# Attention and feed-forward on one core: weighted sums next to the scores, feed-forward work behind them, batches begun a third of a group later, no dummies in batch 0

## Chip, cores, metric

One core of a Trainium2 chip. The metric is device time in microseconds (us); each kernel was run several times and medians are quoted with their ranges. A profile shows one execution, and its span is some 1.8 us shorter than the time of the same run.

## The reference

```python
# q, k, v: (8, 12, 448, 64); batch 8, 12 heads, 448 positions, 64 per head
scores = scale * q @ k^T
m = max(scores);  e = exp(scores - m)
attn = e / (sum(e) + exp(-m) + 1e-9)
x = (attn @ v), heads side by side            # (3584, 768)
h = maximum(maximum(x @ w1, x @ w2), x @ w3)  # three up projections
out = h @ w_out                               # (3584, 768), float32
```

## The kernel before

A *group* is four heads of one batch, so a batch has three groups and there are 24. A group's scores come in seven units, visited in three *visits* of 2, 2 and 3 units. In the first two visits of group i the weighted sums (`av`, e times v) of group i-1 are done too. ScalarE (ACT) takes the exponentials, VectorE (DVE) divides (`xn`) and a DMA transposes the result (`xT`). The feed-forward of a batch is cut into pieces (six matmuls each, or twelve narrower ones); `fill` emits pieces between the attention work, so that TensorE (PE) has work while exponentials run. Batch 0 has nothing to fill with at first: its queries are split into an "E" part (with dummy matmuls) and an "O" part (filled with feed-forward of the E rows).

PSUM, where PE writes, is two pools: three large tiles of two banks for scores and weighted sums, two small ones of one bank for feed-forward pieces:

```python
ps_s = tile_pool(name="ps_s", bufs=3, space=PSUM)   # tiles [128, 2, 512] fp32
ps_b = tile_pool(name="ps_b", bufs=2, space=PSUM)   # tiles [128, 512] fp32
```

The main loop:

```python
for i in range(3, NI):
    ...  # DMA transposes of q, k for group i+2, loads
    if i >= 7 and i % 3 == 1:
        add_batch(i // 3 - 1)              # next batch's pieces, at visit 0
    ...
    for vi, units in enumerate(visits):
        ...
        scores(i, (i + 1) % NEB, units)
        if vi < 2:
            av_tail(i - 1, pj, vi, ws)
        if vi == 0:
            per = share()
        fill(per / 6)
        if vi < 2:
            av_main(i - 1, pj, vi, ws)
        if vi == 1:
            ...
                x_transpose_dma(i - 1)     # xn -> xT, issued from the SP queue
        ...
        fill(per / 6)
        if vi == 2 and i + 1 < PE_QK:
            transpose_pe(i + 1, 0, nc.vector)
            transpose_pe(i + 1, 1, nc.vector)
    if i + 2 < NI and i + 2 >= PE_QK:
        shift_q(i + 2, nc.gpsimd)          # waits for the DMA transpose of q
    prep_v(i, nc.vector if i < PE_QK else nc.gpsimd)   # v for group i's weighted sums
```

The softmax here doesn't subtract the row's maximum and nothing guards it: scores larger than these inputs give would overflow.

## Time and profile before

| | before |
|---|---|
| median of the first three runs | 364.44 us (363.95 to 368.81) |
| span of the profiled run | 360.7 us |
| PE busy | 336.8 us |
| first 448-column scores (group 3) | 46.73 us |
| first matmul of batch 1's feed-forward | 90.54 us |

In the profile page the span is cut into 40 slices (9.0 us each); a digit is the busy share in tenths, PEclk the clock granted to PE. Two rows of the kernel before:

```profile
PE   8899978886999979999799999999999999999994
PEclk9999999999999999999899999999999999999998
```

Apart from the last slice, the lowest PE digits lie in the first ten slices; later single digits 7 stand at borders of batches, and the one 8 in the clock row before the end follows such a border. The chain that ended last, of the same page, by line:

```profile
PE p_i L389 46%; PE op_ps L412 11%; PE avp L319 10%; PE stp L262 9%; DMA xT<-xn 6%; PE avp L302 2%; DMA QT<-ld_q 2%; DMA ld_v<-in_v_dram 2%; ACT e L282 1%; PE trT L170 1%; DVE QT L191 1%; DVE xn L335 1%; DVE KT L189 1%; POOL QT L207 1%; PE warm L155 1%
```

Most is PE's own work (p_i: up projections, op_ps: output projection, avp: weighted sums, stp: scores). What is not is foremost the DMA transpose xT<-xn with 6%. GpSimd's (POOL's) timeline of the kernel before (start us, us, instruction, count, idle before it and what ended it) shows the order behind the 2.6 us wait on vt:

```profile
86.43 2.34 POOL L207 COPY QT<-QT 64x384 f16<-64x384 f16 x4 [8.14 <-DMA QT<-ld_q]
88.83 0.82 POOL L345 COPY vx<-ld_v 128x768 f16<-128x768 f16 x1
89.60 0.29 POOL L347 COPY vt<-ld_v 64x128 f16<-64x128 f16 x1
```

`prep_v` (L345, L347) stands behind `shift_q` (L207), which waited 8.14 us for a DMA that PE did not yet need.

### The profile page before, as it was taken

What the parts mean: (1) busy time and instruction counts of PE and PEld (TensorE: products, weight loads), DVE (VectorE), ACT (ScalarE), POOL (GpSimd) and SP (SyncE); (2) the same over time, 40 slices, a digit from 0 to 9 for tenths busy, and PEclk for the clock granted to TensorE, in tenths of its full rate; (3) what the DMA queues carried; (4) which work ended last, traced back from release to release, by engine and by line L of the source; (5) the groups of instructions that cost most, each with busy time, mean ns of one, the idle gap of its engine ahead of it and who ended that gap; (6) DMA issues with size and microseconds to landing.
All of it is one profiled execution on the core that took longest, in us unless ns stands there. A gap on an engine that the chain in (4) does not pass through costs nothing.

```text
span 360.7 us, 9768 instructions
## 1 busy us (share of the span) xinstructions
PE 336.8 (93%) x4168; PEld 199.3 (55%) x4168; DVE 190.9 (53%) x423; ACT 147.2 (41%) x174; POOL 136.7 (38%) x241
## 2 busy tenths in 40 slices
PE   8899978886999979999799999999999999999994
PEld 3557757753555645555455645555555655565552
DVE  2665556653554636554355545555554655565553
ACT  3672355556245244455243443545445255400000
POOL 8733433153805806273246334636192600000000
PEclk9999999999999999999899999999999999999998
DMA  7999997979999995999986997999999251115006
GB/s 107 198 208 206 206 200 75 125 123 236 135 117 102 168 222 99 115 136 115 204 110 89 143 170 184 131 102 155 199 147 116 69 148 29 32 31 131 2 8 167
DMA packets 89499, 47.42 MB, mean 131 GB/s; under 512 B 58224, under 2 KB 85872, under 8 KB 89456
## 3 DMA queue, kind: packets, MB, share of 16 engines
q0 software_dynamic: 29392, 22.03, 47.4%
q1 hardware_dynamic: 60064, 24.78, 39.6%
q8 instruction: 32, 0.52, 0.7%
q14 instruction: 11, 0.09, 0.1%
HBM read 44.04 MB, written 11.01 MB: 153 GB/s over the span
## 4 chain that ended last, share of the span: by engine, by line
PE 80%; DMA 10%; DVE 4%; POOL 2%; ACT 1%; issue 1%; ACTq 0%; POOLq 0%; DVEq 0%
PE p_i L389 46%; PE op_ps L412 11%; PE avp L319 10%; PE stp L262 9%; DMA xT<-xn 6%; PE avp L302 2%; DMA QT<-ld_q 2%; DMA ld_v<-in_v_dram 2%; ACT e L282 1%; PE trT L170 1%; DVE QT L191 1%; DVE xn L335 1%; DVE KT L189 1%; POOL QT L207 1%; PE warm L155 1%
## 5 line engine op out<-in xcount | busy, mean ns | idle before, releaser
L282 ACT ACTIVATE e<-stp 128x896 f16<-128x896 f32 (+4 forms) x171 | 144.8, 903 | 162.5 <-PE stp L262 162.4
L389 PE MATMUL p_i<-xT,w 128*128 128x448 f16 (+2 forms) x972 | 179.7, 333 | 5.8 <-DMA xT<-xn 5.3
L389 PEld LDWEIGHTS <-w 128*128 128x128 f16 x972 | 87.8, 98 | 71.5 <-issue 13.0
L400 DVE TENSOR_TENSOR hT<-hT,p_i 128x448 f16<-128x448 f16 (+2 forms) x96 | 59.6, 621 | 65.5 <-PE p_i L389 65.5
L207 POOL COPY QT<-QT 64x384 f16<-64x384 f16 (+1 forms) x72 | 39.9, 555 | 125.7 <-DMA QT<-ld_q 120.0
L412 PE MATMUL op_ps<-w,hT 128*128 128x384 f16 x336 | 58.8, 326 | 0.0
L262 PE MATMUL stp<-QT,KT 64*64 64x448 f16 (+2 forms) x756 | 49.1, 339 | 4.4 <-DVE QT L191 2.6
L398 DVE CAST hT<-p_i 128x448 f16<-128x448 f32 (+2 forms) x48 | 30.0, 625 | 40.3 <-PE p_i L389 40.3
L419 DVE TENSOR_SCALAR o_sb<-op_ps 128x384 f32<-128x384 f32 x56 | 31.1, 556 | 29.6 <-PE op_ps L412 29.6
L319 PEld LDWEIGHTS <-e 128*128 128x128 f16 x1152 | 42.3, 98 | 6.8 <-issue 0.2
L319 PE MATMUL avp<-vx,e 128*128 128x65 f16 x1152 | 45.4, 194 | 0.0
L412 PEld LDWEIGHTS <-hT 128*128 128x128 f16 x336 | 31.0, 98 | 21.8 <-issue 2.2
L335 DVE TENSOR_TENSOR xn<-avp,rb 128x512 f16<-128x512 f32 (+1 forms) x54 | 34.1, 632 | 1.9
L262 PEld LDWEIGHTS <-KT 64*64 64x64 f16 x756 | 15.1, 105 | 33.1 <-issue 23.9
L302 PEld LDWEIGHTS <-e 64*64 64x64 f16 x768 | 14.9, 107 | 14.5 <-issue 4.7
L302 PE MATMUL avp<-vt,e 64*64 64x65 f16 x768 | 16.3, 193 | 5.7 <-POOL vt L347 2.6
L103 POOL DMA_DIRECT2D ld_k<-in_k_dram x25 | 17.8, 713 | 4.8 <-DMA w<-in_moe_w_out_dram 1.5
L103 POOL DMA_DIRECT2D ld_q<-in_q_dram x24 | 17.8, 742 | 3.9 <-DMA w<-in_moe_w_dram 1.2
L329 DVE TENSOR_SCALAR rb<-avp 128x8 f32<-128x8 f32 (+1 forms) x54 | 8.9, 164 | 15.0 <-PE avp L319 11.0
L116 POOL DMA_DIRECT2D ld_v<-in_v_dram x24 | 15.2, 634 | 3.4 <-DMA w<-in_moe_w_out_dram 1.6
L113 POOL DMA_DIRECT2D ld_v<-in_v_dram x24 | 15.1, 631 | 2.3 <-DVE xT L368 1.5
L345 POOL COPY vx<-ld_v 128x768 f16<-128x768 f16 x18 | 14.8, 822 | 1.7 <-POOL vt L348 0.7
(32 smaller groups left out, 90.5 us busy)
## 6 DMA issues: line engine op xcount, KB each, us to landing
out_dram<-o_sb SPq DMA_DIRECT2D x56, 192.0 KB, 3.2
ld_v<-in_v_dram POOLq DMA_DIRECT2D x48, 128.0 KB, 5.0
ld_q<-in_q_dram POOLq DMA_DIRECT2D x24, 224.0 KB, 8.0
ld_k<-in_k_dram POOLq DMA_DIRECT2D x23, 224.0 KB, 6.9
w<-in_moe_w_dram POOLq DMA_DIRECT2D x9, 384.0 KB, 12.2
w<-in_moe_w_out_dram POOLq DMA_DIRECT2D x3, 384.0 KB, 11.6
xT<-xn SPq DMA_TRANSPOSE x21, 3.8
QT<-ld_q SPq DMA_TRANSPOSE x18, 6.4
```

Source lines behind the costliest of these rows:

```text
L103: nc.gpsimd.dma_start(out=tiles[nm][:, 1 : NP * T + 1].rearrange("x (r t) d -> x r (t d)", r=NP)[:, p0:p1], in_=src[:, p0:p1],)
L207: eng.tensor_copy(out=t[d0 : d0 + HP, o * 128 : (o + n) * 128], in_=t[s0 : s0 + HP, a * 128 : (a + n) * 128],)
L262: nc.tensor.matmul(out=stp[half * HP : half * HP + HP, par, j * qn : (j + 1) * qn], lhsT=k_block(i, pr, h2, x[half]), rhs=q_cols(i, pr, h2 ...
L282: nc.scalar.activation(out=dst, in_=src, func=AF.Exp, scale=scale)
L302: nc.tensor.matmul(out=ps[half * HP : half * HP + HP, hh, j * D1 : (j + 1) * D1], lhsT=eF[hh * HP : hh * HP + HP, o : o + HP], rhs=vt[hh * ...
L319: nc.tensor.matmul(out=ps[:, hh, j * D1 : (j + 1) * D1], lhsT=eF[:, o : o + 128], rhs=vx[:, 2 * pr + hh, (x[0]), 0:D1], start=False, stop= ...
L335: nc.vector.tensor_tensor(out=xn[i][:, pr, ws[0] : ws[0] + nw].rearrange("p j h d -> p h j d"), in0=acc[:, :, :, 0:D], in1=rb[:, :, 0:nw]. ...
L389: nc.tensor.matmul(out=p_i[:, j * qn : (j + 1) * qn], lhsT=w_sb[i][:, dc, ts(fc, 128)], rhs=xT[b][:, dc, q0 : q0 + qn], start=(dc == 0), s ...
L398: nc.vector.tensor_copy(out=dst, in_=src)
L400: nc.vector.tensor_tensor(out=dst, in0=dst, in1=src, op=ALU.max)
L412: nc.tensor.matmul(out=op_ps[:, 0:NW], lhsT=hT[bp][:, fc, ts(t, 128)], rhs=wout_sb[:, fc, ts(nh, NW)], start=(fc == 0), stop=(fc == NFC - 1),)
L419: nc.vector.tensor_scalar(out=o_sb[:, ts(nh, NW)], in0=op_ps[:, 0:NW], scalar1=1.0 / LAMBDA, scalar2=None, op0=ALU.mult,)
```

## The change

The intent: put a visit's weighted sums next to its scores and let the whole share of feed-forward follow; begin each batch's feed-forward one visit later; prepare v earlier; use the small pool for the transposes of q and k; drop the dummies. Cut to its core:

```diff
 def transpose_pe(i, pr, k_eng):
-    tp = ps_s.tile([128, 2, 1024], ...)                       # large pool
+    tps = [ps_b.tile([128, 1024], ...) for _ in range(2)]     # small pool, one each for k and q
 ...
 # batch 0, E and O parts
-    for u in range(4): scores; av of the part before; transposes; warm(2) in E; fill in O
+    scores 0-3; av 0; transpose_pe(g+1, 0, nc.scalar); fill; scores 4-5; av 1;
+    transpose_pe(g+1, 1, nc.scalar); prep_v; fill; scores 6; fill; x transpose; fill
 ...
+    adds = {3 * (3 * b + 4) + 1: b for b in range(1, B - 1)}   # visit 1, not 0
     for vi, units in enumerate(visits):
+        n = 3 * i + vi
-        scores; av_tail; fill(per / 6); av_main; [x_transpose_dma]; fill(per / 6)
+        scores(i, ej, units)
+        if vi < 2: av(i - 1, pj, vi, ...)                      # tail and main together
+        if vi == 1: prep_v(i, nc.vector if i < PE_QK else nc.gpsimd)
+        if n in adds: add_batch(adds[n])
+        per = share(n)
+        [vi == 1: x_transpose_dma(i - 1)]
+        [vi > 0 and i + 1 < PE_QK: fill(per / 2); transpose_pe(i + 1, vi - 1); fill(per / 2)]
+        [else: fill(per)]
     shift_q(i + 2, nc.gpsimd)
-    prep_v(i, ...)                                             # was here
```

(Lines in brackets are shortened; both versions do the same arithmetic, apart from the dummies.)

More of the change, by code (lines that the diff above doesn't have):

```diff
@@ L166, in transpose_pe @@
     def transpose_pe(i, pr, k_eng):
-        tp = ps_s.tile([128, 2, 1024], MMDT, tag="s", name="trT")
+        tps = [ps_b.tile([128, 1024], MMDT, tag="b", name="trT") for _ in range(2)]
         kr, qr = raw[i]["k"], raw[i]["q"]
@@ L170, in tr @@
             nc.tensor.transpose(
-                out=tp[:, n, ts(j, 128)],
+                out=tps[n][:, ts(j, 128)],
                 in_=src[:, t + 1 : t + 3, :].rearrange("x t d -> x (t d)"),
@@ L184, in transpose_pe @@
             QT[i] = att_pool.tile([P, (NB + 1) * 128], MMDT, tag="QT", name="QT")
-        kd, ks = KT[i][:, kj[0] * 128 : (kj[-1] + 1) * 128], tp[:, 0, 0 : len(kj) * 128]
+        kd, ks = KT[i][:, kj[0] * 128 : (kj[-1] + 1) * 128], tps[0][:, 0 : len(kj) * 128]
         if k_eng is nc.scalar:
@@ L191, in transpose_pe @@
         nc.vector.tensor_copy(
-            out=QT[i][:, q0 : q0 + len(qt) * 128], in_=tp[:, 1, 0 : len(qt) * 128]
+            out=QT[i][:, q0 : q0 + len(qt) * 128], in_=tps[1][:, 0 : len(qt) * 128]
         )
@@ L475, with av @@
     parts = [(part, g) for part in "EO" for g in range(NG)]
-    hu = ((0, 1), (2, 3), (4, 5), (6,))
-    PW = {"E": (0, 1), "O": (2, 3)}
+    PW = {"E": (0, 1), "O": (2, 3), "EO": (0, 1, 2, 3)}
+    def av(i, ej, pr, part):
+        av_tail(i, ej, pr, PW[part])
+        av_main(i, ej, pr, PW[part])
     for n, (part, g) in enumerate(parts):
-        for u in range(4):
-            scores(g, n % NEB, hu[u], part)
-            if n > 0:
-                pp, pg = parts[n - 1]
-                if u in (0, 1):
-                    av_tail(pg, (n - 1) % NEB, u, PW[pp])
-                    av_main(pg, (n - 1) % NEB, u, PW[pp])
-                elif u == 2:
-                    x_transpose_pe(pg, pp)
-                    if pg == NG - 1:
-                        add_up(0, 0, NE, [(i, f) for i in range(2) for f in (0, 2, 4)])
-            if part == "E":
-                if u == 1:
-                    prep_v(g, nc.vector)
-                if u in (2, 3) and g + 1 < NG:
-                    transpose_pe(g + 1, u - 2, nc.vector)
-                if u < 3:
-                    warm(2)
-            else:
-                if g == 2 and u == 1:
-                    add_up(0, 0, NE, [(2, f) for f in (0, 2, 4)])
-                fill(1.2 * UP)
+        ej = n % NEB
+        pp, pg = parts[n - 1] if n > 0 else (None, None)
+        step = 1.2 * UP if part == "O" else 0
+        scores(g, ej, (0, 1), part)
+        scores(g, ej, (2, 3), part)
+        if n > 0:
+            av(pg, 1 - ej, 0, pp)
+        if part == "E" and g + 1 < NG:
+            transpose_pe(g + 1, 0, nc.scalar)
+        fill(step)
+        scores(g, ej, (4, 5), part)
+        if n > 0:
+            av(pg, 1 - ej, 1, pp)
+        if part == "E" and g + 1 < NG:
+            transpose_pe(g + 1, 1, nc.scalar)
+        if part == "E":
+            prep_v(g, nc.vector)
+        fill(step)
+        scores(g, ej, (6,), part)
+        fill(step)
+        if n > 0:
+            x_transpose_pe(pg, pp)
+            if pg == NG - 1:
+                add_up(0, 0, NE, [(i, f) for i in range(2) for f in (0, 2, 4)])
+        fill(step)
         if n == 1:
@@ L508, with share @@
             load_qk(5)
+            transpose_pe(3, 0, nc.vector)
+            add_up(0, 0, NE, [(2, f) for f in (0, 2, 4)])
         if n == 5:
-            transpose_pe(3, 0, nc.vector)
             transpose_pe(3, 1, nc.vector)
     visits = ((0, 1), (2, 3), (4, 5, 6))
+    adds = {3 * (3 * b + 4) + 1: b for b in range(1, B - 1)}
+    def share(n):
+        nxt = min([a for a in adds if a > n], default=3 * NI + 2)
+        return left() / (nxt - n)
     for i in range(3, NI):
-        b, g = groups[i]
+        ej, pj = (i + 1) % NEB, i % NEB
+        first = i == 3
@@ L517 @@
         if i + 2 < NI and i + 2 >= PE_QK:
             transpose_dma(i + 2)
-        if i == 3:
+        if first:
             load_v(5)
             load_qk(6)
-        if i + 3 < NI and i > 3:
+        elif i + 2 < NI:
             load_v(i + 2)
-            load_qk(i + 3)
-        elif i + 2 < NI and i > 3:
-            load_v(i + 2)
-        if i >= 7 and i % 3 == 1:
-            add_batch(i // 3 - 1)
-        per = 0.0
-        def share():
-            nxt = 7 if i < 7 else (i - 1) // 3 * 3 + 4
-            return left() / max(1, nxt - i)
+            if i + 3 < NI:
+                load_qk(i + 3)
@@ L535 @@
         for vi, units in enumerate(visits):
-            first = i == 3
-            pj = i % NEB
-            ws = PW["O"] if first else (0, 1, 2, 3)
-            scores(i, (i + 1) % NEB, units)
+            n = 3 * i + vi
+            scores(i, ej, units)
             if vi < 2:
-                av_tail(i - 1, pj, vi, ws)
-            if vi == 0:
-                per = share()
-            fill(per / 6)
-            if vi < 2:
-                av_main(i - 1, pj, vi, ws)
-            if vi == 1:
-                if first:
-                    x_transpose_pe(i - 1, "O")
-                    add_up(0, NE, NO, [(w, f) for w in range(3) for f in (0, 2, 4)])
-                    add_out(0)
-                else:
-                    x_transpose_dma(i - 1)
@@ L554 @@
-            if first:
-                per = share()
-            fill(per / 6)
-            if vi == 2 and i + 1 < PE_QK:
-                transpose_pe(i + 1, 0, nc.vector)
-                transpose_pe(i + 1, 1, nc.vector)
+                av(i - 1, pj, vi, "O" if first else "EO")
+            if vi == 1:
+                prep_v(i, nc.vector if i < PE_QK else nc.gpsimd)
+            if n in adds:
+                add_batch(adds[n])
+            per = share(n)
+            if vi == 1 and first:
+                fill(per / 2)
+                x_transpose_pe(i - 1, "O")
+                add_up(0, NE, NO, [(w, f) for w in range(3) for f in (0, 2, 4)])
+                add_out(0)
+                per = share(n)
+            elif vi == 1:
+                x_transpose_dma(i - 1)
@@ L560 @@
+            if vi > 0 and i + 1 < PE_QK:
+                fill(per / 2)
+                transpose_pe(i + 1, vi - 1, nc.vector)
+                fill(per / 2)
+            else:
+                fill(per)
         if i + 2 < NI and i + 2 >= PE_QK:
             shift_q(i + 2, nc.gpsimd)
-        prep_v(i, nc.vector if i < PE_QK else nc.gpsimd)
-    av_tail(NI - 1, NI % NEB, 0)
-    av_tail(NI - 1, NI % NEB, 1)
-    av_main(NI - 1, NI % NEB, 0)
-    av_main(NI - 1, NI % NEB, 1)
+    av(NI - 1, NI % NEB, 0, "EO")
@@ L568 @@
+    av(NI - 1, NI % NEB, 1, "EO")
     x_transpose_dma(NI - 1)
```

## The prediction

> **What bounds the kernel now.** I read four views in this order: the page's busy line, a table of stages (busy time by stretch), the waits of TensorE (PE) by stage, and PE's timeline around each wait. First the page's busy line and stages of the table, whose columns are stretch, length, busy us (instructions) of PE, PEld, DVE, ACT, POOL, then granted clock, DMA share, GB/s:
>
> ```profile
> PE 336.8 (93%) x4168; PEld 199.3 (55%) x4168; DVE 190.9 (53%) x423; ACT 147.2 (41%) x174; POOL 136.7 (38%) x241
> ...
> 8.00:23.00 15.00, 13.89 (x234) 8.05 (x237) 10.27 (x34) 10.53 (x12) 9.83 (x15) 1.00 1.26 200
> 23.00:47.00 24.00, 22.11 (x358) 17.27 (x358) 13.41 (x36) 9.17 (x14) 10.17 (x16) 1.00 1.21 206
> 47.00:91.00 44.00, 35.38 (x611) 25.11 (x604) 22.23 (x59) 25.56 (x30) 16.72 (x30) 1.00 1.01 150
> 91.00:130.00 39.00, 39.00 (x479) 22.14 (x477) 21.75 (x44) 16.31 (x20) 20.38 (x36) 1.00 1.24 129
> ...
> 170.00:213.00 43.00, 40.41 (x460) 22.79 (x456) 21.28 (x43) 17.77 (x21) 18.51 (x33) 0.96 0.91 139
> ```
>
> PE is the bound: 336.8 of 360.7 us. Of the 23.9 us that it idles, 1.2 lie at the start and 5.2 at the end (last matmul 355.5), which no part of the change touches. So some 17.5 us of idleness can be won. Half is in 47 to 91 (44.00 - 35.38 = 8.6): batch 0's feed-forward rest under groups 3 to 6. From 91 on each batch runs PE full except where the next batch begins. Whom PE waited for, from 130 on and then in 47 to 91 (us in total, times, longest):
>
> ```profile
> PE p_i L389 <- DMA xT<-xn: 5.3, 3, 2.6
> ```
> ```profile
> PE avp L302 <- POOL vt L347: 2.6, 1, 2.6
> PE avp L302 <- DVE vt L347: 2.0, 3, 0.7
> PE stp L262 <- DVE xn L335: 1.4, 2, 0.7
> PE stp L262 <- DVE QT L191: 1.3, 3, 0.4
> PE xtp L362 <- DVE xn L335: 0.8, 1, 0.8
> ```
>
> PE's timeline at one batch border, and the clock there:
>
> ```profile
> 169.95 0.93 PE L389 MATMUL p_i<-xT,w 128*128 128x448 f16 x4
> 173.47 0.70 PE L389 MATMUL p_i<-xT,w 128*128 128x448 f16 x2 [2.59 <-DMA xT<-xn]
> 173.96 1.53 PE L319 MATMUL avp<-vx,e 128*128 128x65 f16 x24
> 175.30 2.20 PE L389 MATMUL p_i<-xT,w 128*128 128x448 f16 x6
> ```
> ```profile
> 174.00:175.30 1.30, 1.30 (x25) 1.30 (x24) 0.62 (x1) 0.00 (x0) 0.00 (x0) 0.50 1.01 384
> ```
>
> Four matmuls of the new batch run, the fifth waits 2.59 us for the transposed x, and after that wait the clock is halved for some 3 us: the weighted sums take 1.34 us to the next start where they take 0.75 elsewhere, the next six matmuls 2.13 instead of 1.22. So this wait cost 2.59 + 0.6 + 0.9 = 4.1 us.
>
> **What the Trainium skill says.** "TensorE: Matmul & The Clock Gate", Back-to-back issue gap, gives N/2.4 + 2.5 ns: 189 ns for 448 columns. The trace agrees: 18 up-projection matmuls run 3.51 us to the next start and 12 run 2.37, so 190 ns each; nothing is to be won inside the matmuls. The same page, Part 1: The HAM clock gate, says that PE is clocked at half after an idle window of about 3.4 us and recovers after about that time busy. The trace shows the half clock (0.50) after a gap of only 2.59 us, but not after 2.60 at 89.9 nor 2.16 at 133.2, so the page's length is no safe limit here. Its Architectural detail says that ScalarE, VectorE and GpSimd queues are strictly first in, first out; the 2.6 us wait on POOL fits (below). "PSUM — Partial Sum Buffer", PSUM bank collisions raise a hardware error, tells why VectorE and ScalarE must not read one bank at once; here QT's copy waited for ScalarE's KT copy out of the shared tile (6.2 us, twice), and the change gives each its own.
>
> **The change part by part.**
>
> (a) *Weighted sums right behind the scores.* Before, a visit is scores, tail, half the fill, main, half the fill; after, scores, tail, main, whole fill. The instructions are the same. In the timeline the main part takes 0.75 us for 24 matmuls between fills, and two tails and mains back to back at the end 0.38 + 1.52, so 0.95 a visit, against 0.22 + 0.75 = 0.97. A fill starts some 0.08 us late after a main, 0.01 after a tail. Per visit about 0.02, over 42 visits 1 us at most: call it 0.3. What does change is that the fill now covers xn's VectorE chain (0.17 + 0.20 + 0.69): the two 0.7 waits on xn go.
>
> (b) *Each batch a third of a group later.* A group is 13 us, a third 4.3. The wait for xT moves by that, and the transposing DMA is issued half a fill (1.2 us) earlier. The waits were 2.16, 2.59 and 0.58, all below 4.3: all 5.3 us go, and with them the slow clock's 1.5. **6.8 us**, and this stretch has no slack elsewhere to swallow it. At the end, 2/7 of batch 6 instead of 1/3 is left to hide the last transpose: 18,020 of 63,072 columns, 6.4 to 7.5 us, against xn 1.2 + DMA some 3 to 5. Enough.
>
> (c) *prep_v at visit 1.* On VectorE it stood behind the transposes' copies, on POOL behind the shift of QT, which waits for its own DMA (79.1 to 86.4). Now it runs two thirds of a group before its use: 2.6 + 2.0 = **4.6 us** go.
>
> (d) *Transposes into the small pool (two banks), interleaved with fill.* The three 0.43 waits on QT before scores go (1.3). New: the q transposes take the bank of the piece just finished and must wait for its eviction, 0.56 to 0.69 us less the k transposes' 0.17: about 0.45 each, five times, **+2.2 us**.
>
> (e) *Batch 0, E half without dummies.* 18 dummies in 9 pairs of 0.53 us: 4.8 us of PE time in 8 to 23. But they partly fill waits. Without them a group has about 4.0 us of PE work, while ScalarE has 3 exps of 1.02, one of 0.60 and now two KT copies (0.49, 0.60): 4.75 us. So ScalarE becomes the bound: from 8.5, three groups of exps (3.67 each) and two pairs of copies (1.09) end at 21.7, with some 0.7 of bubbles 22.4, against about 23.2 now. **-0.8 us**, not 4.8.
>
> (f) *O half.* Its first pieces still wait for x of the last E group, and now no piece lies between that part's later visits: scores, two av and the x transpose with waits of about 0.45 + 0.8 + 0.3. The pieces begin at 26.3 as now (26.5), with two instead of three done in that part. **About +1 us**: batch 0 up to 47 us comes out even.
>
> (g) *Groups 3 to 6.* PE work up to batch 1: scores 6.4, av 7.9, four transposes 2.6, x transpose 0.4, nine up pieces 9.2, six out pieces 6.1: 32.6 us. Waits that I expect there: transposes 1.8, exps and xn in group 3 (which still has little to fill) 3.0, and 0.7 twice where the seventh exp of a group (7 x 0.865 = 6.1 us a group against 7.0 of PE work) is not out of the third score buffer when the next av wants it: 6.2. Sum 38.8 against 43.9 (46.7 to 90.6) plus the 0.75 of av that stands ahead of batch 1 after but not before: **-5.5 us**. This contains (c), the xn and QT waits of (a) and (d), and the new ones.
>
> Sum: (a) -0.3, (b) -6.8, (e) -0.8, (f) +1, (g) -5.5: **-12.4 us** on 364.4, 352.0. I take 352.5, as the slow clock may strike elsewhere.
>
> **The rivals.** *The small pool becomes the bound.* Transposes, x transposes and pieces share two banks, and each p_i eviction (0.63 of 1.14 us) is already tight; if waits are 1 us per transpose and hit KT's copy on ScalarE too, (d) and (f) grow by 4: 356.5. For it: the 0.16 waits on hT in batch 0. Against: VectorE is only half busy. *PE falls to half clock in the E half.* Its density falls to some 80%; a few windows at half clock would cost 3 to 6 us: 356 to 358. Against: no single gap there should exceed 1 us. *Loads bound batch 0.* DMA moves 200 to 206 GB/s up to 47 us, and group 1's k arrives about 10.2; then (e) yields nothing, 353. *The dummies were pure cost:* if the copies fit into ScalarE's gaps, (e) yields 3: 350. *The POOL chain of loads, shift and prep_v binds in faster groups 5 to 7:* shift of group 7 done 73.3 + 2.4, loads 2.7, prep_v 1.4 gives 79.8, needed about 81: no wait, but near; 0 to 2 us.
>
> **Range and chances.** (b) is nearly sure and alone gives 1.9%; (g) can lie between -2 and -8, (e) + (f) between -3 and +4. That gives 347 to 359. Faster by over 2% means below 357.2: 0.83. Within 2%: 0.16. Slower: 0.01.
>
> **What would show it.** (b): no wait of PE on xT, clock 1.00 from 130 to 350, batches 38 to 40 us. (c): no wait on vt. (d): waits of q transposes on hT, near 0.45. (e): scores of the O half begin about 22, ScalarE over 85% busy from 9 to 22. (f): group 3 begins at 46 to 47.5. (g): batch 1 begins near 86. I am wrong if waits on the small pool or the third score buffer exceed 1 us each, if the clock falls in the first 25 us, or if PE's busy time in the full batches changes: then adjacent sums cost or save more than (a) says.

## The result

The changed kernel took 352.1 us (median of 4 runs, 351.23 to 352.71) against 364.19 (4 runs, 360.58 to 368.81) for the kernel before. The ratio is 0.9698, 95% interval 0.9623 to 0.9773: faster. Such a ratio is the mean time of one kernel's fast runs over that of the other's of the same rounds, so it is not quite the ratio of the medians. The forecast was 352.5.

Rows of the changed kernel's page that answer to those of before (slices of 8.75 us):

```profile
PE 331.4 (95%) x4150; PEld 198.8 (57%) x4150; DVE 190.5 (54%) x419; ACT 148.4 (42%) x178; POOL 136.8 (39%) x241
...
PE   7789879799999999999999999999999999999994
...
PEclk9899999999999999999999999999999999999999
...
PE p_i L389 47%; PE op_ps L412 15%; PE avp L319 11%; PE stp L262 11%; ACT e L282 3%; PE avp L302 2%; DMA ld_q<-in_q_dram 2%; PE trT L170 2%; DVE hT L400 1%; POOL ld_k L103 1%; PE xtp L362 0%; DVE xn L335 0%; DVE xT L368 0%; DVE rb L332 0%; DVE QT L191 0%
```

PE is full from the eleventh slice to the last but one, and xT<-xn has left the chain. A new low stands in the clock row: the second slice. The changed kernel's table by stretch (columns as in the prediction), cut at its own batch borders:

```profile
8.00:23.00 15.00, 11.90 (x220) 8.40 (x215) 7.96 (x27) 12.35 (x17) 9.37 (x14) 0.89 1.25 194
23.00:47.00 24.00, 21.18 (x347) 17.35 (x346) 13.68 (x37) 8.33 (x12) 10.28 (x16) 1.00 1.21 206
47.00:89.30 42.30, 36.74 (x682) 26.83 (x681) 24.30 (x62) 26.24 (x32) 20.35 (x35) 1.00 1.06 150
89.30:128.90 39.60, 39.60 (x486) 22.44 (x483) 21.93 (x44) 17.95 (x23) 18.55 (x34) 1.00 1.10 166
128.90:166.50 37.60, 37.60 (x475) 21.29 (x472) 20.80 (x42) 17.99 (x23) 18.51 (x33) 1.00 0.98 145
```

From 89.3 us PE does not idle at all until its last matmul, and the waits view lists no wait of PE there. From 47 to 89.3 it still idles 5.6 us:

```profile
PE trT L170 <- DVE hT L400: 1.8, 2, 1.4
PE avp L302 <- ACT e L282: 0.9, 2, 0.4
PE xtp L362 <- DVE xn L335: 0.8, 1, 0.8
PE stp L262 <- ACT e L282: 0.8, 2, 0.4
PE trT L170 <- DVE hT L398: 0.5, 1, 0.5
PE p_i L389 <- DVE xT L368: 0.3, 1, 0.3
```

None of these is on vt (the waits that went); those of trT on hT, of a transpose on the eviction of a feed-forward piece, are new.

**Where the 10.7 us between the two profiles went.** I follow the same point of the work in both. The O half's first scores begin at 23.05 before and 22.95 after: -0.10. Group 3 begins at 46.73 and 47.04, so the O half took 24.09 instead of 23.68, 0.41 longer. Batch 1's feed-forward begins at 89.31 after; before it begins at 90.54, but there some 2.1 us of attention work (one main part 0.75, scores 0.40, a tail and a main 0.97) follow which the changed kernel has already done, so the like point is 92.7. Groups 3 to 6 thus took 45.97 before and 42.27 after: -3.7. From there to the end it is 360.7 - 92.7 = 268.0 against 350.0 - 89.3 = 260.7: -7.3. The sum is -0.10 + 0.41 - 3.7 - 7.3 = -10.7.

### The profile page after: what moved, and what is told of

It reads as the page before. It is cut to its first block, busy times and chain, and to the rows that moved or that the text cites. A ratio compares the mean times of both kernels' runs of the same rounds, so it can differ in the third digit from the quotient of the medians.

```text
span 350.0 us, 9732 instructions
## 1 busy us (share of the span) xinstructions
PE 331.4 (95%) x4150; PEld 198.8 (57%) x4150; DVE 190.5 (54%) x419; ACT 148.4 (42%) x178; POOL 136.8 (39%) x241
## 4 chain that ended last, share of the span: by engine, by line
PE 89%; DVE 3%; ACT 3%; DMA 2%; issue 2%; POOL 1%; ACTq 0%; POOLq 0%
PE p_i L389 47%; PE op_ps L412 15%; PE avp L319 11%; PE stp L262 11%; ACT e L282 3%; PE avp L302 2%; DMA ld_q<-in_q_dram 2%; PE trT L170 2%; DVE hT L400 1%; POOL ld_k L103 1%; PE xtp L362 0%; DVE xn L335 0%; DVE xT L368 0%; DVE rb L332 0%; DVE QT L191 0%
## 5 line engine op out<-in xcount | busy, mean ns | idle before, releaser
L389 PE MATMUL p_i<-xT,w 128*128 128x448 f16 (+2 forms) x972 | 173.7, 332 | 1.1 <-DVE hT L400 0.6
L389 PEld LDWEIGHTS <-w 128*128 128x128 f16 x972 | 89.7, 98 | 69.1 <-issue 6.3
L400 DVE TENSOR_TENSOR hT<-hT,p_i 128x448 f16<-128x448 f16 (+2 forms) x96 | 59.6, 621 | 44.3 <-PE p_i L389 44.1
L319 PEld LDWEIGHTS <-e 128*128 128x128 f16 x1152 | 39.0, 97 | 2.5 <-issue 0.3
L262 PEld LDWEIGHTS <-KT 64*64 64x64 f16 x756 | 16.1, 106 | 26.0 <-issue 21.8
L103 POOL DMA_DIRECT2D ld_q<-in_q_dram x24 | 17.8, 744 | 4.1 <-PE stp L262 1.7
L116 POOL DMA_DIRECT2D ld_v<-in_v_dram x24 | 15.2, 635 | 3.2 <-DMA ld_q<-in_q_dram 2.2
L113 POOL DMA_DIRECT2D ld_v<-in_v_dram x24 | 15.2, 632 | 2.3 <-DMA w<-in_moe_w_dram 1.5
```

Source lines behind the costliest of these rows:

```text
L103: nc.gpsimd.dma_start(out=tiles[nm][:, 1 : NP * T + 1].rearrange("x (r t) d -> x r (t d)", r=NP)[:, p0:p1], in_=src[:, p0:p1],)
L262: nc.tensor.matmul(out=stp[half * HP : half * HP + HP, par, j * qn : (j + 1) * qn], lhsT=k_block(i, pr, h2, x[half]), rhs=q_cols(i, pr, h2 ...
L319: nc.tensor.matmul(out=ps[:, hh, j * D1 : (j + 1) * D1], lhsT=eF[:, o : o + 128], rhs=vx[:, 2 * pr + hh, (x[0]), 0:D1], start=False, stop= ...
L389: nc.tensor.matmul(out=p_i[:, j * qn : (j + 1) * qn], lhsT=w_sb[i][:, dc, ts(fc, 128)], rhs=xT[b][:, dc, q0 : q0 + qn], start=(dc == 0), s ...
L400: nc.vector.tensor_tensor(out=dst, in0=dst, in1=src, op=ALU.max)
```

## The experiments

All outputs are right. Three calls of four kernels, each with its own runs of the kernel before. Those runs scattered: 360.4 to 376.3 in the first call, 359.0 to 371.1 in the second, 357.0 to 380.8 in the third. A run over 1.5% above its kernel's fastest counts as slow and is left out of ratios, so in the third call only one run of before was left and no ratio could be given. The changed kernel itself was run again.

### x1_later_only: the later beginning alone

```diff
 # kernel before
-        if i >= 7 and i % 3 == 1:
-            add_batch(i // 3 - 1)
         for vi, units in enumerate(visits):
+            n = 3 * i + vi
+            if n in adds:                # adds = {3 * (3 * b + 4) + 1: b}
+                add_batch(adds[n])
```
(and the share of fill is computed by visit, as in the changed kernel)

> The kernel before with one part of the change: each batch's feed-forward is begun one visit later. My step (b): PE's three waits on xT (5.3 us) and the half clock after them (1.5 us) go, the waits in groups 3 to 6 (some 8 us) stay: span near 353.9 in the profile against 360.7, ratio 0.98. Rival: the wait only moves to the new beginning, or PE then waits for something else there: the waits on xT stay above 3 us, ratio above 0.99.

Measured: 356.19 us (354.62 to 359.96), ratio 0.9874 (0.977 to 0.9978). In its profile (span 352.8, clock 0.998) PE has no wait on xT, and the stretch that had the half clock is full:

```profile
170.00:213.00 43.00, 43.00 (x528) 24.32 (x526) 24.16 (x49) 19.40 (x24) 21.78 (x39) 1.00 0.96 167
```

From group 3's first scores to the end: 352.8 - 47.7 = 305.1 against 314.0 before, 8.9 less. Of that 6.8 were expected; the wait on POOL's vt, which also shrank from 2.6 to 0.6 in this run, makes up the rest. The step holds. The ratio of the times is smaller (1.3%), with an interval that spans 0.2 to 2.3%.

### x3_prepv_only: the earlier prep_v alone

```diff
 # kernel before
             if vi == 1:
+                prep_v(i, nc.vector if i < PE_QK else nc.gpsimd)
 ...
-        prep_v(i, nc.vector if i < PE_QK else nc.gpsimd)
```

> The kernel before with prep_v moved from the end of a group to visit 1 and nothing else. My step (c): PE's waits on vt (2.6 us on POOL, 2.0 us on VectorE) go and nothing takes their place in that kernel: 4 to 5 us, ratio 0.987. Rival: the same instants are bound by the last exponentials and the third score buffer as well, and the waits turn into waits on ACT: less than 2 us, ratio above 0.994.

Measured: 360.79 us (353.07 to 363.76), ratio of the two fast runs 0.9822 (0.9675 to 0.997). In the profile no wait on vt is left, and from group 3 to batch 1's first matmul it takes 86.22 - 47.55 = 38.7 us against 43.8 before: 5.1 less, as expected. But the waits on xT stay:

```profile
PE p_i L389 <- DMA xT<-xn: 4.6, 2, 2.8
```

With them stays the scatter of 10 us: the fastest run, 353.07, is as short as those of the next kernel, so the waits on xT do not cost the same in every run.

### x9_later_prepv: both together, nothing else

Edit: the two diffs above in one kernel.

> The kernel before with two parts of the change together, the later beginning (b) and the earlier prep_v (c), and nothing else: transposes stay in the large pool, dummies stay, sums stay split around the fill. Theory: these two are the whole gain and the rest of the change nets to nothing, so from the first 448-column scores to the end this takes 302 to 304 us, as the changed kernel does (303.0, before 314.0), ratio near 0.97. Rival: the sums next to the scores carry part of it as well (clearing xn and the score buffers earlier): then 306 us or more, ratio above 0.98.

Measured: 352.98 us (351.33 to 354.32), against 352.36 (351.48 to 354.03) of the changed kernel; from group 3's scores to the end 351.2 - 47.6 = 303.6 us. The means of the six fast runs of each are 352.81 and 352.41: the same within 0.1%. So these two parts are the whole gain in time. What the other parts bring and cost nets to nothing.

### after_again: the changed kernel once more

> The changed kernel as it is, once more, as the measure for the others of this call: median 351 to 353, ratio 0.965 to 0.975, no run above 355, whereas the kernel before spreads over more than 8 us because each of its waits on xT can halve the clock. If its runs spread as widely, the spread has another cause than these waits.

Measured: 352.36 us, no run above 354.03; ratio 0.9763 (0.9685 to 0.9841) to only three fast runs of before out of eleven. The absolute forecast was met; the upper end of the ratio's forecast (0.975) was missed by 0.001, because only the three fastest runs of before count in it. The changed kernel and x9_later_prepv scatter over some 3 us, the kernel before and x3_prepv_only over 10 or more, which fits waits on xT that now and then halve the clock. But x8_rearranged and x12_split_sums (below), which have no such waits in their profiles, scattered over 10 and 7 us, so another cause of scatter remains, and the point is not settled.

### x2_after_early: the changed kernel with the early beginning

```diff
-    adds = {3 * (3 * b + 4) + 1: b for b in range(1, B - 1)}
+    adds = {3 * (3 * b + 4): b for b in range(1, B - 1)}
```

> The changed kernel with that one part undone: each batch begins at visit 0 of its group as before, everything else as changed. If the later beginning alone removes the xT waits, they come back: 5.3 us and more with the clock, span near 356 to 357. Rival: the transposing DMA, now issued half a fill (1.2 us) earlier, and the weighted sums (0.75 us) now ahead of the fill already take 1.95 us off each wait; of 2.16, 2.59 and 0.58 us there remain 0.2, 0.6 and 0: span near 351, no half clock.

Measured: 359.62 us (359.41 to 361.07), span 359.3. That is even above the first theory, and the mechanism is neither's. PE's timeline at the border of batches 1 and 2, then the table there:

```profile
125.80 0.92 PE L319 MATMUL avp<-vx,e 128*128 128x65 f16 x24
131.98 6.39 PE L389 MATMUL p_i<-xT,w 128*128 128x448 f16 x18 [5.26 <-DVE o_sb L419]
```
```profile
132.00:134.00 2.00, 2.00 (x6) 0.85 (x6) 1.36 (x4) 0.00 (x0) 0.00 (x0) 0.50 0.26 66
```

This profile is of the slowest of the four runs (361.07). PE waited 5.26 us for a small bank that held an output piece. VectorE could not evict it, because all three output buffers were still being stored:

```profile
131.37 1.02 DVE L419 TENSOR_SCALAR o_sb<-op_ps 128x384 f32<-128x384 f32 x2 [7.48 <-DMA out_dram<-o_sb]
```

From 110 to 135 us stores took 9.6 us to land (median), against 4.5 us in the changed kernel in the same stretch; xT took 10.2. Then the clock fell to half (18 matmuls in 6.39 us, 3.57 elsewhere). 5.3 + 2.8 us, and 0.9 + 0.6 of smaller waits, come to 9.6 us, against 9.3 between the spans. So in the changed kernel the early beginning costs no less than before: 9.3 us by the profiles, some 7.5 by the medians (of two calls), against 7.3 ("The result").

### x11_early_outbufs: the same with six output buffers

```diff
-    out_pool = tile_pool(name="outp", bufs=3)
+    out_pool = tile_pool(name="outp", bufs=6)      # on top of x2_after_early
```

> The changed kernel with the early beginning of batches, as in the run that lost 7 us, but with six output buffers instead of three. There PE waited 5.3 us at the border of batches 1 and 2, put down to VectorE's eviction, which itself waited 7.5 us for a store that took 10.5 us; xT of the last group landed 2 to 3 us earlier than that store. If the output buffers were the cause alone, the wait goes wholly: 353 us. If xT is late as well, as the crowded DMA engines suggest, 2 to 3 us of wait on xT stay, with a half clock behind it: 355 to 357.

Measured: 355.72 us (351.79 to 358.31); the four fast runs have a mean of 354.2, so most of the loss went with the buffers. The profiled run is slow. In it the 5.3 us wait is gone and this stays:

```profile
PE p_i L389 <- DMA xT<-xn: 3.0, 2, 2.2
```

In that run, then, xT was late too; whether it was in the fast ones no trace shows. That crowded DMA engines delay both is argued, not shown: they moved no more in x2_after_early than in the changed kernel (153 and 164 GB/s from 110 to 135 us), but the eight stores of the batch follow one another there, where the changed kernel has four and four. Beginning later removed the wait on xT in every profile; one on the stores (1.2 us) stayed in x9_later_prepv.

### x6_big_pool: transposes back in the large pool

```diff
-        tps = [ps_b.tile([128, 1024], MMDT, tag="b", ...) for _ in range(2)]
+        tp = ps_s.tile([128, 2, 1024], MMDT, tag="s", ...)
+        tps = [tp[:, 0], tp[:, 1]]
```

> The changed kernel with the transposes of q and k back in one tile of the large pool. My step (d): the waits of transposes on hT (in its profile 3.5 us in six places) go, and since a tile of that pool is free after each fill little takes their place: 2 to 3 us faster than the changed kernel. Rival: they then wait for exponentials in the large pool, and in the first 20 us VectorE waits again for ScalarE's copy of the other half: no gain, or slower by up to 2 us.

Measured: 350.33 us (349.15 to 353.06), 2.0 less than the changed kernel. Where the waits came from, in the changed kernel's timelines (PE, then DVE):

```profile
62.69 0.33 PE L170 MATMUL trT<-ident,ld_k 128*128 128x128 f16 x3
64.39 0.61 PE L170 MATMUL trT<-ident,ld_q 128*128 128x128 f16 x8 [1.37 <-DVE hT L400]
```
```profile
62.94 0.35 DVE L345 COPY vx<-ld_v 128x768 f16<-128x768 f16 x1
63.21 0.33 DVE L347 COPY vt<-ld_v 64x128 f16<-64x128 f16 x1
63.55 0.19 DVE L348 COPY vt<-ld_v 64x128 f16<-64x128 f16 x1
63.78 0.56 DVE L400 TENSOR_TENSOR hT<-hT,p_i 128x384 f16<-128x384 f16 x1
```

The q transposes need the bank of the piece that just ended, and its eviction (63.78) stands on VectorE behind prep_v's three copies, which this same change moved there. In x6_big_pool no transpose waits on hT; the O half takes 23.36 us instead of 24.09, groups 3 to 6 take 41.2 instead of 42.3. The rival's wait in the first 20 us came as well (each of the six QT copies waits for ScalarE's copy), but cost less than this gain.

### x8_rearranged and x10_combined: other orders

x8 in short:

```diff
+    # group 0: scores 4-5 first, then warm(6), then group 1's transposes
+    # last O part: transposes of group 3 behind its scores; x transpose ahead of the fill
+    # groups 3 and 4: transpose_pe right behind the scores, then av, then the whole fill
+    W = (0.7, 0.7, 1.6) if n < 21 else (1.0, 1.0, 1.0)     # weights of the visits' fill
```

> The changed kernel rearranged in four places: transposes of groups 4 and 5 directly behind a visit's scores instead of between two fills, those of group 3 behind scores of the last O part, x's transpose ahead of the fill; six dummies and one scores call put into the gap in which group 1's q is still being loaded; in groups 3 to 6 the third visit gets 1.6 parts of the fill and the others 0.7. Theory: PE's waits in batch 0 are order, not bound: of 3.5 us on hT by transposes, 1.8 on ACT, 0.6 on p_i and some 1.6 of half clock at least 4 us go, span 344 to 346.5, ratio near 0.957. Rival: these waits are bound by VectorE's and ScalarE's latency and only move: span 348.5 or more.

Measured: 350.12 us (347.99 to 357.93), five fast runs with a mean of 349.63 against 352.41 of the changed kernel; span 347.8. The gain lies in groups 3 to 6, 39.8 us instead of 42.3. It is less than expected: 2 us, since waits on ACT stay (2.4 us). With scores and six dummies in the gap in front of group 1's transposes the clock stayed at 1.00 from 8 to 23 us.

x10 has the large pool too, with transposes at the end of a visit's fill:

> The changed kernel with what paid so far: transposes of q and k in the large pool at the end of a visit's fill, x's transpose ahead of the fill, the third visit of a group given more fill in groups 3 to 6, group 1's transposes behind the scores and six dummies. If the gains of the large pool (2.0 us) and of the rearrangement (2.2 us) add: 348 us or less. Rival: both remove the same waits: 350 us.

Measured: 350.8 us (350.08 to 353.1). It was run at another time. The gains do not add, but the rival's reason explains only a part. The waits of transposes on hT are gone here, as they are in x6 and nearly in x8 (0.5 us). Groups 3 to 6, however, take 42.4 us, longer than in x6 (41.2) and x8 (39.8): it has 2.3 us of waits on QT (1.7 in x6, none in x8) and a clock of 0.79 from 47 to 55 us. So a better mixture is not ruled out. By the means of fast runs x6 is 0.5% and x8 0.8% faster than the changed kernel (x10 0.3%): these beat both kernels, but by little against the scatter, and which of the three is best the runs don't decide.

### x5_no_dummies and x4_dummies_back

x5 takes the dummies from the kernel before (the line `if u < 3: warm(2)`), x4 puts `warm(2)` three times into each E part of the changed kernel.

> The kernel before without the 18 dummy matmuls of batch 0 (the 10 at the start stay). If they are pure cost, 4.8 us of PE time go: the O half's first scores begin at 18.3 instead of 23.1 us. My step (e) and what the changed kernel's profile shows (half clock from 12 to 15 us after a 1.6 us wait on q's load): the stretch is bound by loads, VectorE's and ScalarE's copies, so at most 1 us goes, and the clock falls to half somewhere between 10 and 16 us: ratio 0.997 to 1.003.

Measured: 364.04 us (356.24 to 369.58). Only one run was fast and the profiled one was slow, so the time decides nothing. In that profile the clock is 0.77 from 8 to 23 us, as expected; the O half's scores still begin at 23.48, not at 18.3. Its first scores were late (9.18, before 8.02), so this E half took 14.3 us instead of 15.0: the expected gain of at most 1 us, if a slow run may be read so.

> The changed kernel with the 18 dummies of the E half put back, two behind each of a part's first three stretches of scores. My reading of step (e): in the E half the changed kernel waits for group 1's q and then runs at half clock for some 3 us, bound by ScalarE; dummies fill the wait and hold the clock (8 to 23 us: 1.00 instead of 0.77 to 0.89), which repays most of their 4.8 us: same time within 1 us of 352.4. Rival: they are pure cost, and with ScalarE's chain already tight they delay it: 355 or more.

Measured: 354.66 us (353.33 to 357.96), 2.3 over after_again. It was run at another time. This went against my expectation. In this profile the clock was half from 9.3 to 12.7 us (first line, 10 to 12 us), but it fell before the first of these dummies (9.79), behind a wait of 1.80 us on group 0's k; so whether dummies hold the clock was not tested here. They wait themselves, since they take banks of the small pool behind the transposes (second line, waits view):

```profile
10.00:12.00 2.00, 2.00 (x17) 0.86 (x16) 0.00 (x0) 1.48 (x2) 1.03 (x2) 0.50 1.31 195
```
```profile
PE warm L155 <- ACT KT L187: 1.3, 3, 0.7
```

From the first scores to the O half it took 27.05 - 9.24 = 17.8 us, against 15.2 and 16.5 in the two profiles of the changed kernel, and against 13.3 in three others that run the same code up to there and whose first scores were as late (below, (e)). In the new order and at these places the dummies are cost, nearly all of their 4.8 us.

### x12_split_sums: the sums split around the fill again

```diff
-            if vi < 2: av(i - 1, pj, vi, ...)
+            if vi < 2: av_tail(...)
+            fill(per)                  # per = share(n) / 2
+            if vi < 2: av_main(...)
 ...
-            fill(per)                  # per = share(n)
+            fill(per)                  # the other half
```

> The changed kernel with the weighted sums split around half of the fill again, as before, and all else kept. My step (a): some 0.02 us a visit over 42 visits, so under 1 us slower in the full batches, plus the waits on xn and score buffers in groups 3 to 6 (0.7 twice): 352.5 to 354.5 against 352.4. Rival: neighbouring small matmuls are slower than separated ones (each must load its own weights): then it is faster by 2 us or more, 350.

Measured: 355.66 us (352.89 to 359.89), over the expected range by 1.2 us. Its profiled run is its fastest, 352.89; there waits on xn are back as foreseen,

```profile
PE avp L302 <- DVE xn L335: 1.4, 2, 0.7
```

and the full batches show no idle PE. At like points (batch 1's first matmul comes before a main part of 0.75 us here) groups 3 to 6 take 44.1 us against 42.3 in the changed kernel, the rest 260.5 against 260.7. So in this profile adjacent sums gain 1.8 us in groups 3 to 6 and nothing in the full batches. What its other five runs lost, no trace shows; the neighbouring call may differ too. It speaks against the rival (350 us).

## Why the prediction was right

The time (352.5 forecast, 352.1 measured) was right, and so was the main mechanism; the sizes of (d), (e) and (g) missed by 0.7 to 1.8 us in these profiles. Two of the signs that the prediction had named for being wrong did come: a wait on the small pool above 1 us (1.37) and a half clock in the first 25 us. Neither cost enough to overturn the result.

- **(a) Adjacent sums: no gain to be seen in the full batches.** The step gave them 0.02 us a visit. The batch of the kernel before that had no wait takes 39.74 us (252.14 to 291.88), the changed kernel's 39.6; x12_split_sums, with the sums split, has 260.5 us for all that follows, against 260.7. The gain is in groups 3 to 6, through the waits on xn, as the step also said.
- **(b) Later beginning, 6.8 us: right.** The like-for-like rest after batch 1's start fell by 7.3 us. From start to start the three waits cost 2.33, 4.26 (with the half clock) and 0.75, together 7.3, so nothing is left over for (a). x1_later_only shows it alone. What I did not see is that the early beginning would be no cheaper in the changed kernel, by another wait (x2_after_early).
- **(c) prep_v, 4.6 us: right.** x3_prepv_only gives 5.1 us in that stretch.
- **(d) Small pool, +2.2 us: right in kind, too small.** The profile shows 3.5 us in five waits. Four of them, 0.42 to 0.61, are near the 0.45 of the term; the fifth is 1.37, because the term left out what can stand ahead of the eviction on VectorE: prep_v's copies (0.87 us).
- **(e) E half, -0.8 us: off in this pair of profiles.** It gained 0.10. The rivals I had named, the load and the clock, both struck. In the changed kernel's timeline:

```profile
10.67 0.62 PE L170 MATMUL trT<-ident,ld_q 128*128 128x128 f16 x8 [1.58 <-DMA ld_q<-in_q_dram]
...
13.33 1.28 PE L262 MATMUL stp<-QT,KT 64*64 64x256 f16 x20
```
```profile
13.00:14.00 1.00, 1.00 (x20) 0.70 (x21) 0.56 (x2) 0.48 (x2) 0.59 (x2) 0.50 1.39 193
```

  The step that failed is "Against: no single gap there should exceed 1 us": the transposes of group 1 were moved ahead of scores 4-5, into the time in which q was still being loaded. But this depends on when the loads land. Three more profiles run the same code up to here (x2_after_early, x11_early_outbufs, x12_split_sums); group 0's k landed later in them, q then held PE for 0.2 us at most, and the E half took 13.3 us. In x12_split_sums, whose first scores begin at 9.10, the O half begins so:

```profile
22.41 0.53 PE L262 MATMUL stp<-QT,KT 64*64 64x192 f16 x16
```

  Over five profiles the O half begins at 22.3 to 24.1 (mean 22.9), with the old order and dummies over four (before, x1, x3, x9) at 23.05 to 24.06 (mean 23.7). So the step's 0.8 us is about right on average, and one pair of profiles was too few to see it.
- **(f) O half, about +1 us: right in sign**, 0.41 measured (the O half takes 23.68 us in all five profiles with the old order, 24.09 or 24.10 in the six with the new one and the small pool); batch 0 ended at 47.04, within "46 to 47.5".
- **(g) Groups 3 to 6, -5.5 us: too large.** It was -3.7. (By its own sum the step should read -5.85: 38.8 against 43.9 + 0.75.) "PE work up to batch 1 ... 32.6 us" left out visit 1 of group 7 (1.4 us), which the changed kernel does before batch 1. This accounts for 1.4 of the 3.3 us by which "Batch 1 begins near 86" failed (89.3), but not for the gain, since the 44.65 us of before leave it out too. The term that was mis-sized is PE's work: it was busy for 36.7 us there, against 32.6 + 1.4 = 34.0, and idle for 5.6 against the 6.2 of the waits. A part of it is waiting that counts as busy: a wait costs some 0.17 us more from start to start than its idle time (the three on xT before: 2.16, 2.59 and 0.58 us idle, 2.33, 2.76 and 0.75 lost), and there are nine waits in the view. How the rest divides stays open.
- **Two readings.** QT's copy waited 6.2 us for ScalarE's copy of KT, but 5.70 of this is VectorE's idle time before the first loads had landed; ScalarE's two copies take 0.49 and 0.60 us. And the skill's section gives N/2.4 + 2.5 ns for an isolated matmul and says that it over-counts in a stream at large N; here the stream's 190 ns agree with it all the same.

The sum of the steps was -12.4 us. The profiles differ by 10.7, the medians by 12.1, because the profiled run of before was faster than its median. The hit of the median to 0.4 us is thus partly luck; within the profiles the error is 1.7 us: (g) and (e) fell short by 1.8 and 0.7, while (f) cost 0.6 less and (a) with (b) gave 0.2 more.

## What to carry to other kernels

When a transfer stands between two stages, do not only look at how long it takes: ask which other work could run until it lands, and begin the dependent work one step later if there is enough of it; here no wait came in its place in the changed kernel, and both the waits and the half clock behind them went. An in-order engine that waits for something early delays what is needed now, so put the copy with the near deadline ahead of the one that waits. When a change of order moves work into a smaller pool or onto an engine queue, count what stands ahead of the evictions there. And where a stage starts with loads, look at several profiles before judging a change smaller than their spread (here the first scores began between 7.6 and 9.3 us).

## What the Trainium skill lacked or had wrong

- "TensorE: Matmul & The Clock Gate", Part 1: The HAM clock gate, tells of an idle window of about 3.4 us before the clock is halved, and the page's table under Why this matters for your kernels asks for no gaps over some 3 us. Here 2.59 us of waiting was followed by 0.50 in the kernel before (2.60 elsewhere was not). In the changed kernel 1.58 us (1.65 in after_again) was followed by 0.50 for some 3 us (6 us), but only 1.0 to 1.3 us after the gap had ended. From 8.8 to 11.2 us PE did nothing but transposes there, and no run shows whether the gap or this kind of work was what counted.
- "DMA: Bandwidth & Descriptors", Issuing engines are not separate DMA queues, says that all queues run on the same 16 engines and interleave. No run here isolates that, but the delays fit, and that section has no size for them: at a batch border stores landed in 9.6 us (x2_after_early) instead of 4.5 (the changed kernel), and one such store held PE for 5.26 us through three output buffers.
- "Perfetto Trace Analysis", Tensor Engine Instruction, calls the end of a matmul's row estimated. That section does not say what this does to idle times: here a wait cost some 0.17 us more from start to start than the idle time shown (2.76 against 2.59).
